# A K projection in two bank halves, and second scores and sums moved among the V quarters

## The chip, the cores and the metric

The kernel runs on one core of one Trainium2 chip. The metric is the device time of one execution in microseconds (us); before the change it was 892.15 us, the median of three runs (890.42 to 892.38).

## The reference, cut to what matters

The block has two parts. Part A is a segment-recurrent attention over 2048 tokens of width 512, with 32 heads of size 128. It walks through 64 segments of 32 tokens; each sees eight memory rows and its own tokens, and its first eight output rows are the memory of the next segment, so the segments must be done one after the other. Part B is a gated feed-forward block with a spatial mixing over all 2048 tokens. The attention loop is what matters here:

```
for s in range(n_seg):
    h = concat([mem, x[:, 32*s : 32*s+32]])      # 40 rows
    q, k, v = h @ Wq, h @ Wk, h @ Wv             # 32 heads of 128
    scores = where(mask, q @ k.T * scale, -1e9)
    p = softmax(scores)
    o = (p @ v) @ Wo
    mem = o[:, :8]
    outs.append(o[:, 8:])
```

## The kernel before

The kernel is a list of instructions for five engines, written out by hand in `fast_path`. A small emitter tracks which instruction reads and writes which token (a tile, or one of the eight PSUM banks) and places the semaphore waits; the order on each engine is the order of the calls. There is no scheduler: where a call stands in the step loop (line 869) is where its instructions stand in the queues of TensorE, ScalarE and VectorE.

The weights stay in SBUF. The projections of a step have only 32 rows, so each matmul uses a 128x32 column tile of the array, and four matmuls in four column tiles run side by side (the text calls them a quad). One projection of 16 heads is four quads of 512 columns, one for each 128 of the model width (`dc`). The step loop handles the heads in two halves, `b` 0 and 1:

- `QK(s, b, mi)` (L474) projects q (`mi` 0) or k (`mi` 1) of half `b` into bank 0, 1, 6 or 7 (`QKB`, L462). `QK_evac` (L485) copies the bank with ScalarE into `Tst` (L488), and VectorE transposes it in 32x32 blocks into `QT` (L494) or `KT` (L497).
- `S_half(s, b)` (L507) computes the scores into bank `b`: four mask matmuls (L511), which need no data of the step, then sixteen for the heads (L520) and four for the memory rows (L526).
- `sm_exp` (L532) is the exponential, `sm_sums` (L537) sums it with a matrix of ones (L541, L546), `sm_ln` (L553) and `sm_rcp` (L557) make the reciprocal on ScalarE, and `sm_norm` (L561, L566) multiplies it in on VectorE.
- `V_half(s, b, dcs)` (L569) projects v into bank 6 or 2; its four quads, one for each `dc`, are the V quarters, 0 to 3. `V_evac` (L579) copies the result, half 0 with VectorE (L584), half 1 with ScalarE (L582).
- `PV_half(s, b)` (L586) multiplies probabilities and values (L592, and L598 for the memory rows) into banks 0, 1, 6 and 7. Then follow `cT_evac` (L607), the output projection `Wo` (L619, matmuls L625), its copies `part_evac` (L636, ScalarE half L640), and `mem_out` (L644, matmuls L649), which brings the eight memory rows into the next step's `hT`.

Between the V quarters and PV stands a filler group of other work, where there is one (L942): in step 0 to 47 a group that prepares a later chunk, which is a V group of four quads (`vx_group`, L430) in steps 0 to 7, 14 and 15 and a Q or K group of sixteen 128x128 matmuls (L411) otherwise; in steps 49 to 62 a piece of part B's input projection (`z2_pre`, L725). Steps 48 and 63 have none.

The part of the step loop that the change touches reads before (arguments as in the code):

```
QK(s, 1, mi); QK_evac(s, 1, mi)      # mi = 0, then 1
S_half(s, 0); sm_exp(0)
V_half(s, 0); V_evac(0, "dve")       # four quarters
sm_sums(0); sm_ln(0)
S_half(s, 1); sm_exp(1); sm_rcp(0)
V_half(s, 1, (0, 1, 2))
sm_sums(1); sm_ln(1); sm_rcp(1)
V_half(s, 1, (3,)); V_evac(1, "act")
sm_norm(0); sm_norm(1)
```

Of the kernel before, what the change touches and what calls it, by code (L numbers as in the profile page):

```python
# [8 lines left out]
U32 = mybir.dt.uint32  # L9
# [160 lines left out]
def fast_path(nc, st, keep, A_x, A_mem0, A_Wq, A_Wk, A_Wv, A_Wo, A_seg_len, B_w_in, B_w_sp, B_b_sp, B_w_out, out):  # L170
# [9 lines left out]
    DC = D // 128  # L180
# [85 lines left out]
    def PB(b):  # L266
        return ("ps", b)
# [10 lines left out]
    def dve(fn, **k):  # L278
        return em.add("dve", fn, **k)
# [101 lines left out]
    def slot(s):  # L381
        return s % NSLOT
# [91 lines left out]
    def QK(s, b, mi, dcs=range(DC)):  # L474
# [3 lines left out]
        for dc in dcs:  # L478
            for c in range(4):
# [2 lines left out]
                                                           start=(dc == 0), stop=(dc == DC - 1), tile_position=(0, 32 * c)),  # L482
                   reads=[("hTx", (s // 4) % 3), ("hTm", s, dc // 2), ("W", mi, 2 * b), ("W", mi, 2 * b + 1)], writes=[PB(bank)])

    def QK_evac(s, b, mi):  # L485
        bank = QKB[(b, mi)]
        tb = mi
        act(lambda e: e.activation(out=Tst[:, tb, :].rearrange("p (hp i r) -> p hp i r", i=32, r=2),  # L488
                                   in_=ps[:, bank, :].rearrange("p (hp r i) -> p hp i r", r=2, i=32), func=ACT.Copy),
            reads=[PB(bank)], writes=[("T", tb)])  # L490
        src = Tst[:, tb, :].bitcast(U32)
        if mi == 0:
            dst = QT[:, b, :, :, :].rearrange("p hp q r -> p (hp q r)").bitcast(U32).rearrange("p (hp q) -> p hp q", hp=8)[:, :, 8:40]
            dve(lambda e: e.transpose(out=dst, in_=src), reads=[("T", tb)], writes=[("QT", b)])  # L494
        else:
            dst = KT[:, b, :, :, :].rearrange("p hp q r -> p (hp q r)").bitcast(U32)
            dve(lambda e: e.transpose(out=dst, in_=src), reads=[("T", tb)], writes=[("KT", b)])  # L497

    def qx_copy(s):
        j = s % CK  # L500
# [6 lines left out]
    def S_half(s, b):  # L507
        bank = SBK[b]
        for c in range(4):
            q = slice(32 * c, 32 * c + 32)  # L510
            pe(lambda e, q=q, c=c: e.matmul(ps[q, bank, 0:224], lhsT=ident[:, q], rhs=mask[:, :], start=True, stop=False,  # L511
                                            skip_group_check=True, tile_position=(0, 32 * c)),
               reads=["ident", "mask"], writes=[PB(bank)])
        j = s % CK
        buf = (s // CK) % 2
        rd = [("QT", b), ("KT", b), ("QTe", b)]
        for g in range(4):
            for c in range(4):
                hp, r = 2 * c + g // 2, g % 2
                pe(lambda e, hp=hp, r=r, c=c, g=g: e.matmul(  # L520
                    ps[32 * c:32 * c + 32, bank, g * 40:(g + 1) * 40], lhsT=KT[:, b, hp, :, r], rhs=QT[:, b, hp, :, r],
                    start=False, stop=(g == 3), skip_group_check=True, tile_position=(0, 32 * c)),
                    reads=rd, writes=[PB(bank)])
        for c in range(4):
            h0 = 16 * b + 4 * c
            pe(lambda e, c=c, h0=h0: e.matmul(  # L526
                ps[32 * c:32 * c + 32, bank, 160:224], lhsT=QTx[buf][:, 1, j, h0:h0 + 4, :].rearrange("p h k -> p (h k)"),
                rhs=QT[:, b, 2 * c:2 * c + 2, 0:16, :].rearrange("p hp q r -> p hp r q"),
                start=False, stop=True, skip_group_check=True, tile_position=(0, 32 * c)),
                reads=rd + [("QTx", buf, 1, i) for i in range(8)], writes=[PB(bank)])  # L530

    def sm_exp(b):  # L532
        bank = SBK[b]
        act(lambda e: e.activation(out=E_sb[:, b, :], in_=ps[:, bank, 0:224], func=ACT.Exp, scale=scale, bias=SHIFT),
            reads=[PB(bank)], writes=[("E", b), ("Ex", b)])
# [333 lines left out]
    for s in range(NSEG):  # L869
        j4 = s % 4  # L870
        rb = s // 4
        if j4 == 0 and rb > 0:
            load_h(rb - 1)
        if s == NSEG - 1:
            load_h(rb)
        if s % 2 == 1 and s // 2 < NWT:
            wT_piece(s // 2)
        if j4 == 0 and 2 <= rb + 2 < RB:
            load_x(rb + 2, 0)
        if s == 4:  # L880
            load_xe(3, 1)

        QK(s, 0, 0, (0, 1))
        if s > 0:
            mem_out(s - 1, 1)
        QK(s, 0, 1, (0, 1))
        QK(s, 0, 0, (2, 3))
        QK_evac(s, 0, 0)
        QK(s, 0, 1, (2, 3))
        QK_evac(s, 0, 1)  # L890
        for mi in range(2):
            QK(s, 1, mi)
            lastop["qk"[mi]] = em.by_eng["pe"][-1]
            QK_evac(s, 1, mi)
        if s == NSEG - 1:
            load_wT(0, [lastop["q"]])
        if s == 0:
            for n in range(2):
                start_v(n)
        S_half(s, 0)  # L900
        sm_exp(0)
        if s == 0:
            for n in range(2, 4):
                start_v(n)
        V_half(s, 0)
        V_evac(0, "dve")
        sm_sums(0)
        sm_ln(0)
        S_half(s, 1)
        lastop["s"] = em.by_eng["pe"][-1]  # L910
        sm_exp(1)
        sm_rcp(0)
        if s == 0:
            for n in range(4, 8):
                start_v(n)
        V_half(s, 1, (0, 1, 2))
        sm_sums(1)
        sm_ln(1)
        sm_rcp(1)
        V_half(s, 1, (3,))  # L920
        lastop["v"] = em.by_eng["pe"][-1]
        if s == NSEG - 1:
            sp(lambda e: e.dma_start(w_in1, winr[:, :, 0:FH]), writes=["w_in1"], after=[lastop["s"], lastop["x"]])
            sp(lambda e: e.dma_start(z2[:, 0:NP, :], z2p_d.rearrange("r p f -> p r f")),
               reads=[("z2p", r, hf) for r in range(NP) for hf in range(2)],
               writes=[("z2", r, hf) for r in range(NP) for hf in range(2)], after=[lastop["v"]])
            for r in range(8, RB - 2):
                xn2T_dma(r, [lastop["s"], lastop["x"]])
# [48 lines left out]
        if s == 8:  # L977
            ln_apply(1)
        if s == 12:
            xT(1, XB)  # L980
            late.append(lambda: xe_copy(3, XB))
        elif j4 == 0:
            late += gv.pour(1)
        if j4 == 1 and rb > 0:
            F_group(rb - 1, XB, True)
            F_add(rb - 1, XB)
        if j4 == 2 and 2 <= rb + 2 < RB:
            xT(0, XB)
            late.append(lambda: ring_copy(rb + 2, XB))
        for f in late:  # L990
            f()
        if s + 2 < NSEG:
            load_vx(s + 2)
        if j4 == 1 and rb >= 2:
            xn2_apply(rb - 2, rb % 2)
            xn2_store(rb - 2, rb % 2)
        if s == 3 * CK - 1:
            free0 = [lastop["s"], px]
            sp(lambda e: e.dma_start(w_in2, winr[:, :, FH:F]), writes=["w_in2"], after=free0)
        if 0 <= s - 3 * CK + 1 < 8:  # L1000
            xn2T_dma(s - 3 * CK + 1, free0)
        px = lastop.get("x")
# [956 lines left out]
```

## Time and profile before

| | |
|---|---|
| median of three runs | 892.15 us (890.42 to 892.38) |
| the profiled execution | 891.1 us |
| its span, first to last instruction | 889.4 us |
| mean granted TensorE clock | 0.994 |
| L481, the Q and K projections, busy | 240.5 us, 4096 matmuls |
| L575, the V projections, busy | 140.4 us, 2048 matmuls |
| L488, the Q and K evacuations on ScalarE, busy | 145.9 us, 256 instructions of 596 ns |
| L520, the scores, busy | 35.5 us, 2048 matmuls |
| L541 and L546, the sums, busy | 32.6 and 26.2 us |

The 64 steps take most of the span: the first scores of step 1 start at 63.68 us and those of step 63 at 708.31 us. Busy time on TensorE counts each matmul until its end, while the next one has long started. To see what one costs in a stream, take the distance between starts of successive rows in the timeline; a gap of a tenth of a microsecond does not show as idle time there.

### The profile page before, as it was taken

How to read it: one execution, taken by the hardware profiler on the slowest of the kernel's cores; microseconds unless marked ns; L12 is line 12 of the kernel's file. 1: busy time of each engine (PE TensorE's matmuls, PEld its weight loads, DVE VectorE, ACT ScalarE, POOL GpSimd, SP SyncE). 2: the span in 40 equal slices, each digit the busy share in tenths (PEclk: the TensorE clock that was granted, in tenths of full speed). 3: DMA queues.
4: the chain of work that ended last, by engine and by line, in shares of the span. 5: the costliest groups of instructions: out<-in, count | busy, mean ns of one | idle time of the engine just before them, and what ended most of it. 6: DMA issues, size and time to landing. Idle time of an engine off the chain costs nothing.

```text
span 889.4 us, 46102 instructions
## 1 busy us (share of the span) xinstructions
PE 862.0 (97%) x21213; PEld 487.0 (55%) x21213; DVE 487.4 (55%) x1127; ACT 455.5 (51%) x1145; POOL 110.7 (12%) x280
## 2 busy tenths in 40 slices
PE   6889999999999999999999999999999979999997
PEld 6645555555656555656665655555555534444443
DVE  3445556565656556565656565555555546464443
ACT  2346566666665666666665666565566655400000
POOL 1420111111111111010101111111101013100000
PEclk9999999999999999999999999999999999999999
DMA  9962222222320311211212122432221296032101
GB/s 326 376 180 52 63 57 60 43 60 63 60 58 25 83 45 37 60 54 43 60 42 57 49 61 79 73 73 67 65 61 56 76 273 227 1 100 76 62 13 38
DMA packets 106312, 74.55 MB, mean 84 GB/s; under 512 B 62360, under 2 KB 91616, under 8 KB 106112
## 3 DMA queue, kind: packets, MB, share of 16 engines
q1 hardware_dynamic: 105600, 71.27, 28.8%
q8 instruction: 168, 2.75, 1.3%
q14 instruction: 32, 0.26, 0.1%
q0 software_dynamic: 192, 0.20, 0.1%
q10 hardware_dynamic: 320, 0.07, 0.0%
HBM read 41.07 MB, written 20.22 MB: 69 GB/s over the span
## 4 chain that ended last, share of the span: by engine, by line
PE 93%; DVE 2%; DMA 2%; issue 1%; POOL 1%; ACT 0%; SPq 0%; DVEq 0%
PE f_ps L481 26%; PE f_ps L625 13%; PE f_ps L575 12%; PE f_ps L1064 11%; PE f_ps L411 7%; PE f_ps L676 4%; PE f_ps L592 3%; PE f_ps L430 3%; PE f_ps L1153 3%; PE f_ps L1057 2%; PE f_ps L725 2%; PE f_ps L520 2%; PE f_ps L541 1%; PE f_ps L511 1%; DMA f_arena<-in_B_w_in_dram 1%; PE f_ps L649 1%
## 5 line engine op out<-in xcount | busy, mean ns | idle before, releaser
L481 PE MATMUL f_ps<-f_arena,f_hT 128*32 128x512 bf16 x4096 | 240.5, 380 | 1.0 <-issue 0.4
L488 ACT ACTIVATE f_Tst<-f_ps 128x512 bf16<-128x512 f32 x256 | 145.9, 596 | 78.6 <-PE f_ps L481 78.3
L481 PEld LDWEIGHTS f_ps<-f_arena,f_hT 128*32 128x32 bf16 x4096 | 93.6, 96 | 104.6 <-ACT f_hT L654 33.3
L575 PE MATMUL f_ps<-f_arena,f_hT 128*32 128x512 bf16 x2048 | 140.4, 378 | 0.0
L625 PE MATMUL f_ps<-f_arena,f_cT 128*32 128x256 bf16 x4096 | 127.4, 272 | 0.8 <-ACT f_cT L611 0.8
L625 PEld LDWEIGHTS f_ps<-f_arena,f_cT 128*32 128x32 bf16 x4096 | 99.8, 96 | 24.1 <-ACT f_cT L611 22.1
L494 DVE STREAM_TRANSPOSE f_QT<-f_Tst 128x256 uint32<-128x256 uint32 x128 | 57.0, 445 | 92.4 <-ACT f_Tst L488 92.4
L1064 PE MATMUL f_ps<-f_arena 128*128 128x512 bf16 x448 | 100.1, 379 | 0.0
L613 DVE TENSOR_SCALAR f_cT<-f_ps 128x320 bf16<-128x320 f32 x128 | 56.9, 486 | 39.7 <-PE f_ps L598 39.7
L497 DVE STREAM_TRANSPOSE f_KT<-f_Tst 128x256 uint32<-128x256 uint32 x128 | 57.0, 445 | 29.1 <-ACT f_Tst L488 26.3
L1064 PEld LDWEIGHTS f_ps<-f_arena 128*128 128x128 bf16 x448 | 43.7, 98 | 52.6
L411 PE MATMUL f_ps<-f_hTe,f_arena 128*128 128x128 bf16 x1024 | 68.2, 225 | 4.2 <-DVE f_arena L422 3.2
L411 PEld LDWEIGHTS f_ps<-f_hTe,f_arena 128*128 128x128 bf16 x1024 | 60.6, 101 | 14.1 <-issue 9.2
L504 POOL COPY f_QT<-f_arena 128x256 bf16<-128x256 bf16 x64 | 30.8, 481 | 298.7 <-PE f_ps L526 298.6
L611 ACT ACTIVATE f_cT<-f_ps 128x320 bf16<-128x320 f32 x128 | 49.0, 435 | 36.8 <-PE f_ps L598 36.8
L561 DVE SCALAR_TENSOR_TENSOR f_E_sb<-f_R_sb,f_E_sb 128x160 bf16<-128x160 f32 x128 | 41.6, 325 | 46.3 <-ACT f_R_sb L557 46.3
L642 DVE CAST f_part<-f_ps 128x256 bf16<-128x256 f32 x64 | 27.2, 424 | 67.0 <-PE f_ps L625 67.0
L553 ACT ACTIVATE f_R_sb<-f_ps 128x160 f32<-128x160 f32 x128 | 38.8, 303 | 38.1 <-PE f_ps L546 38.1
L575 PEld LDWEIGHTS f_ps<-f_arena,f_hT 128*32 128x32 bf16 x2048 | 45.1, 95 | 21.1
L654 ACT ACTIVATE f_hT<-f_ps 128x16 bf16<-128x16 f32 x126 | 23.1, 183 | 55.4 <-PE f_ps L649 55.1
L633 POOL COPY f_cTx<-f_cT 128x256 bf16<-128x256 bf16 x64 | 25.6, 401 | 195.6 <-DVE f_cT L613 195.6
L1070 DVE TENSOR_TENSOR f_arena<-f_ps,f_arena 128x512 f32<-128x512 f32 x28 | 19.3, 689 | 55.8 <-PE f_ps L1064 55.8
(106 smaller groups left out, 1160.3 us busy)
## 6 DMA issues: line engine op xcount, KB each, us to landing
wT_d<-f_wst SPq DMA_DIRECT2D x32, 256.0 KB, 2.1
f_arena<-wT_d SPq DMA_DIRECT2D x32, 256.0 KB, 5.1
f_arena<-in_A_Wq_dram SPq DMA_DIRECT2D x4, 1024.0 KB, 8.5
f_arena<-in_A_Wk_dram SPq DMA_DIRECT2D x4, 1024.0 KB, 14.1
f_arena<-in_A_Wv_dram SPq DMA_DIRECT2D x4, 1024.0 KB, 14.5
f_arena<-in_A_Wo_dram SPq DMA_DIRECT2D x4, 1024.0 KB, 13.6
f_Vx<-vext_d SPq DMA_DIRECT2D x62, 64.0 KB, 2.8
vext_d<-f_Vs SPq DMA_DIRECT2D x24, 128.0 KB, 2.0
```

The lines of the kernel that those rows point to most:

```text
L411: pe(lambda e, h=h, dc=dc, hh=hh: e.matmul(ps[:, bank, hh * 128:(hh + 1) * 128], lhsT=ws[:, dc, h * DH:(h + 1) * DH], rhs=hTe[:, ck % 3, d ...
L481: pe(lambda e, dc=dc, c=c, rhs=rhs: e.matmul(ps[32 * c:32 * c + 32, bank, :], lhsT=hT[:, sl, dc, :], rhs=rhs, start=(dc == 0), stop=(dc == ...
L488: act(lambda e: e.activation(out=Tst[:, tb, :].rearrange("p (hp i r) -> p hp i r", i=32, r=2), in_=ps[:, bank, :].rearrange("p (hp r i) -> ...
L494: dve(lambda e: e.transpose(out=dst, in_=src), reads=[("T", tb)], writes=[("QT", b)])
L497: dve(lambda e: e.transpose(out=dst, in_=src), reads=[("T", tb)], writes=[("KT", b)])
L553: act(lambda e: e.activation(out=R_sb[:, b, :], in_=ps[:, bank, 224:384], func=ACT.Ln, scale=LNS), reads=[PB(bank)], writes=[("R", b)])
L561: dve(lambda e: e.scalar_tensor_tensor(out=E_sb[:, b, 0:160], in0=R_sb[:, b, :], scalar=RK, in1=E_sb[:, b, 0:160], op0=ALU.mult, op1=ALU.m ...
L575: pe(lambda e, dc=dc, c=c, c0=c0: e.matmul(ps[32 * c:32 * c + 32, bank, :], lhsT=hT[:, sl, dc, :], rhs=w_v[:, dc, c0:c0 + 512], start=(dc ...
L611: act(lambda e: e.activation(out=dst, in_=src, func=ACT.Copy, scale=UNSC), reads=[PB(PVB[c])], writes=[("cT", c)])
L613: dve(lambda e: e.tensor_scalar(out=dst, in0=src, scalar1=UNSC, scalar2=None, op0=ALU.mult), reads=[PB(PVB[c])], writes=[("cT", c)])
L625: pe(lambda e, h=h, g=g, i=i, b=b, c=c: e.matmul(ps[32 * g:32 * g + 32, bank, 0:d1 - d0], lhsT=cTh[:, i, 8:40], rhs=w_o[:, h, d0:d1], star ...
L1064: pe(lambda e: e.matmul(ps[:, bank, 0:TB], lhsT=z2[:, sc, fb * 128:(fb + 1) * 128], rhs=wTb[tb % 2][:, :, sc, :], start=(n == 0), stop=(n ...
```

## The change

The last projection of each step, K of half 1, is done in two pieces of eight heads. Each piece has four quads of 256 columns, a bank of its own (7 and 2), an evacuation of 256 columns and a transpose of 128 elements, each with its own token; the second scores read both tokens. The first V half is interrupted after three quarters: first sums, second scores, then quarter 3 and the first V evacuation. Of the second V half, two quarters stand in front of the second sums instead of three, and two behind.

```diff
+    KP = (7, 2)
+
+    def K_piece(s, p):
+        bank = KP[p]
+        sl = slot(s)
+        for dc in range(DC):
+            for c in range(4):
+                rhs = w_k[:, dc, :].rearrange("p (h c i) -> p c h i", c=4, i=32)[:, c, 16 + 8 * p:24 + 8 * p, :]
+                pe(lambda e, dc=dc, c=c, rhs=rhs: e.matmul(ps[32 * c:32 * c + 32, bank, 0:256], lhsT=hT[:, sl, dc, :], rhs=rhs,
+                                                           start=(dc == 0), stop=(dc == DC - 1), tile_position=(0, 32 * c)),
+                   reads=[("hTx", (s // 4) % 3), ("hTm", s, dc // 2), ("W", 1, 2 + p)], writes=[PB(bank)])
+        act(lambda e: e.activation(out=Tst[:, 1, 256 * p:256 * p + 256].rearrange("p (hp i r) -> p hp i r", i=32, r=2),
+                                   in_=ps[:, bank, 0:256].rearrange("p (hp r i) -> p hp i r", r=2, i=32), func=ACT.Copy),
+            reads=[PB(bank)], writes=[("T", 1, p)])
+        src = Tst[:, 1, 256 * p:256 * p + 256].bitcast(U32)
+        dst = KT[:, 1, 4 * p:4 * p + 4, :, :].rearrange("p hp q r -> p (hp q r)").bitcast(U32)
+        dve(lambda e: e.transpose(out=dst, in_=src), reads=[("T", 1, p)], writes=[("KT", 1, p)])
...
-        rd = [("QT", b), ("KT", b), ("QTe", b)]
+        rd = [("QT", b), ("QTe", b)] + ([("KT", 1, 0), ("KT", 1, 1)] if b else [("KT", 0)])
...
-        for mi in range(2):
-            QK(s, 1, mi)
-            lastop["qk"[mi]] = em.by_eng["pe"][-1]
-            QK_evac(s, 1, mi)
+        QK(s, 1, 0)
+        lastop["q"] = em.by_eng["pe"][-1]
+        QK_evac(s, 1, 0)
+        for p in range(2):
+            K_piece(s, p)
+        lastop["k"] = em.by_eng["pe"][-1]
...
-        V_half(s, 0)
-        V_evac(0, "dve")
+        V_half(s, 0, (0, 1, 2))
         sm_sums(0)
         sm_ln(0)
         S_half(s, 1)
         lastop["s"] = em.by_eng["pe"][-1]
         sm_exp(1)
+        V_half(s, 0, (3,))
+        V_evac(0, "dve")
         sm_rcp(0)
...
-        V_half(s, 1, (0, 1, 2))
+        V_half(s, 1, (0, 1))
         sm_sums(1)
         sm_ln(1)
         sm_rcp(1)
-        V_half(s, 1, (3,))
+        V_half(s, 1, (2, 3))
```

The rest of the diff splits the token of `Tst` in two halves, so that the other evacuations write, and their transposes read, both.

More of the change, by code (lines that the diff above doesn't have):

```diff
@@ L489, in QK_evac @@
                                    in_=ps[:, bank, :].rearrange("p (hp r i) -> p hp i r", r=2, i=32), func=ACT.Copy),
-            reads=[PB(bank)], writes=[("T", tb)])
+            reads=[PB(bank)], writes=[("T", tb, 0), ("T", tb, 1)])
         src = Tst[:, tb, :].bitcast(U32)
@@ L493, in QK_evac @@
             dst = QT[:, b, :, :, :].rearrange("p hp q r -> p (hp q r)").bitcast(U32).rearrange("p (hp q) -> p hp q", hp=8)[:, :, 8:40]
-            dve(lambda e: e.transpose(out=dst, in_=src), reads=[("T", tb)], writes=[("QT", b)])
+            dve(lambda e: e.transpose(out=dst, in_=src), reads=[("T", tb, 0), ("T", tb, 1)], writes=[("QT", b)])
         else:
             dst = KT[:, b, :, :, :].rearrange("p hp q r -> p (hp q r)").bitcast(U32)
-            dve(lambda e: e.transpose(out=dst, in_=src), reads=[("T", tb)], writes=[("KT", b)])
+            dve(lambda e: e.transpose(out=dst, in_=src), reads=[("T", tb, 0), ("T", tb, 1)], writes=[("KT", b)])
     def qx_copy(s):
```

## The prediction

> **What bounds the kernel now.** The page comes first: how full TensorE is, and who owns the chain that ends last.
>
> ```profile
> span 889.4 us, 46102 instructions
> PE 862.0 (97%) x21213; PEld 487.0 (55%) x21213; DVE 487.4 (55%) x1127; ACT 455.5 (51%) x1145; POOL 110.7 (12%) x280
> PE 93%; DVE 2%; DMA 2%; issue 1%; POOL 1%; ACT 0%; SPq 0%; DVEq 0%
> ```
>
> TensorE owns the end. Its 97% says little about small waits, since a matmul is drawn until its modelled end while the next already runs. So I read the starts in TensorE's timeline. Step 35 is typical of the 64. Four matmuls in four column tiles start together; I call them a quad.
>
> ```profile
> 414.85 3.22 PE L481 MATMUL f_ps<-f_arena,f_hT 128*32 128x512 bf16 x56
> 417.89 0.27 PE L511 MATMUL f_ps<-f_mask,f_ident 128*32 128x224 bf16 x4
> ...
> 418.09 0.20 PE L526 MATMUL f_ps<-f_QT,f_arena 128*32 128x64 bf16 x4
> 418.12 1.04 PE L575 MATMUL f_ps<-f_arena,f_hT 128*32 128x512 bf16 x16
> 419.02 0.25 PE L541 MATMUL f_ps<-f_E_sb,f_ones 128*32 128x160 bf16 x4
> ...
> 419.12 0.27 PE L511 MATMUL f_ps<-f_mask,f_ident 128*32 128x224 bf16 x4
> 419.25 0.28 PE L520 MATMUL f_ps<-f_QT,f_KT 128*32 128x40 bf16 x16
> 419.36 0.20 PE L526 MATMUL f_ps<-f_QT,f_arena 128*32 128x64 bf16 x4
> 419.39 0.82 PE L575 MATMUL f_ps<-f_arena,f_hT 128*32 128x512 bf16 x12
> 420.05 0.25 PE L541 MATMUL f_ps<-f_E_sb,f_ones 128*32 128x160 bf16 x4
> ...
> 420.15 0.39 PE L575 MATMUL f_ps<-f_arena,f_hT 128*32 128x512 bf16 x4
> 420.48 0.51 PE L411 MATMUL f_ps<-f_hTe,f_arena 128*128 128x128 bf16 x6
> ```
>
> The 14 quads from 414.85 to 417.89 take 0.217 us each. The V quads take 0.216. So there are three small waits in this stretch. The first four V quads last 0.90 instead of 0.864: sums 0 waits 0.03 for its exponential. The second scores last 0.27 (419.12 to 419.39), the first 0.23 (417.89 to 418.12): 0.04 for the second K transpose. The second sums wait under 0.01 (0.66 against 0.65). ScalarE and VectorE confirm the first two.
>
> ```profile
> 417.25 0.60 ACT L488 ACTIVATE f_Tst<-f_ps 128x512 bf16<-128x512 f32 x1 [0.21 <-PE f_ps L481]
> 418.12 0.60 ACT L488 ACTIVATE f_Tst<-f_ps 128x512 bf16<-128x512 f32 x1 [0.27 <-PE f_ps L481]
> 418.61 0.35 ACT L534 ACTIVATE f_E_sb<-f_ps 128x224 bf16<-128x224 f32 x1
> ```
> ```profile
> 417.88 0.45 DVE L494 STREAM_TRANSPOSE f_QT<-f_Tst 128x256 uint32<-128x256 uint32 x1 [0.36 <-ACT f_Tst L488]
> 418.75 0.45 DVE L497 STREAM_TRANSPOSE f_KT<-f_Tst 128x256 uint32<-128x256 uint32 x1 [0.42 <-ACT f_Tst L488]
> 419.21 0.69 DVE L584 CAST f_V_sb<-f_ps 128x512 bf16<-128x512 f32 x1
> ```
>
> The exponential ends at 418.96, and sums 0 starts at 419.02. The K transpose ends at 419.20, and the second scores' L520 starts at 419.25. The exponential starts with no idle time before it: it queued behind the K evacuation, though its scores could have reached it at about 418.35 (L526's 418.09 + 0.20, and 0.06 to reach ScalarE; from the last K matmul's end, 414.85 + 3.22 = 418.07, to its evacuation it is 0.05).
>
> A larger wait stands behind it, in steps whose filler group before PV is short. There PV's second half starts late.
>
> ```profile
> 577.52 0.27 PE L592 MATMUL f_ps<-f_E_sb,f_V_sb 32*128 32x40 bf16 x16
> 577.65 0.21 PE L598 MATMUL f_ps<-f_E_sb,f_Vx 32*128 32x64 bf16 x4
> 577.87 0.28 PE L592 MATMUL f_ps<-f_E_sb,f_V_sb 32*128 32x40 bf16 x16
> ```
> ```profile
> 576.90 0.34 ACT L557 ACTIVATE f_R_sb<-f_R_sb 128x160 f32<-128x160 f32 x1
> 577.14 0.58 ACT L582 ACTIVATE f_V_sb<-f_ps 128x512 bf16<-128x512 f32 x1
> ```
> ```profile
> 67.26 0.21 PE L598 MATMUL f_ps<-f_E_sb,f_Vx 32*128 32x64 bf16 x4
> 67.48 0.28 PE L592 MATMUL f_ps<-f_E_sb,f_V_sb 32*128 32x40 bf16 x16
> ...
> 555.91 0.21 PE L598 MATMUL f_ps<-f_E_sb,f_Vx 32*128 32x64 bf16 x4
> 556.68 0.28 PE L592 MATMUL f_ps<-f_E_sb,f_V_sb 32*128 32x40 bf16 x16 [0.56 <-DVE f_E_sb L566]
> ```
> ```profile
> 400.87 0.21 PE L598 MATMUL f_ps<-f_E_sb,f_Vx 32*128 32x64 bf16 x4
> 401.00 0.28 PE L592 MATMUL f_ps<-f_E_sb,f_V_sb 32*128 32x40 bf16 x16
> ```
> ```profile
> PEld f_ps L592 <- issue: 9.6, 25, 0.4
> ```
>
> Undisturbed, the halves lie 0.13 apart (400.87 to 401.00); here it is 0.22 (577.65 to 577.87, and 67.26 to 67.48), a wait of 0.09. The second V evacuation ends at 577.72; 0.05 of signalling and a weight load of about 0.1 later the matmuls start. The list of waits calls this "issue", 25 times. That fits the program: 14 steps with a z2 group, 9 of the first 16 with a V group (step 0 left aside), and 2 with nothing (48 and 63), where the gap is 0.77, so 0.64 too much.
>
> **The change part by part.**
>
> *The K projection in two pieces*: 4 quads of 512 columns become 8 of 256, with 16 more matmuls and 16 more weight loads per step. The output projection runs the same shape with the same 128x32 weights:
>
> ```profile
> 401.89 1.70 PE L625 MATMUL f_ps<-f_arena,f_cT 128*32 128x256 bf16 x56
> 403.43 0.21 PE L649 MATMUL f_ps<-f_G_sb,f_part 128*32 128x8 bf16 x8
> ```
>
> 14 quads in 1.54 is 0.110 each. Before: 4 x 0.217 = 0.87; after: 8 x 0.110 = 0.88, +0.01 per step. K starts at 414.85 + 10 x 0.217 = 417.02, so the pieces finish issuing at 417.46 and 417.90.
>
> *The evacuations.* One of 512 becomes two of 256, on ScalarE ahead of the first exponential.
>
> ```profile
> L640 ACT ACTIVATE f_part<-f_ps 128x256 bf16<-128x256 f32 x64 | 24.5, 383 | 46.0 <-PE f_ps L625 46.0
> ```
>
> A 256-wide one lasts 0.38. Followed at once by another instruction, a 512-wide one occupies the engine for 0.49 of its 0.60 (418.12 to 418.61), an overlap of 0.10. I take 0.28 for 256; without overlap it is 0.38. ScalarE is free of the Q evacuation at 417.25 + 0.49 = 417.74. Piece 0 is there before that (last quad 417.35 + 0.01; a 256-wide matmul lasts 1.70 - 13 x 0.110 = 0.27; then 0.06: 417.69), so it goes 417.74 to 418.12. Piece 1 is there at 417.79 + 0.01 + 0.27 + 0.06 = 418.13 and goes to 418.51; the engine is free at 418.41. The scores reach it at 418.36. So the first exponential starts at 418.41, not 418.61, and ends at 418.76.
>
> *V quarter 3 moved behind the second scores.* Sums 0 now has three V quads ahead of it: 418.13 + 0.65 = 418.78, while the exponential is through at 418.76 + 0.05 or 0.06 = 418.82. The wait is 0.04, about 0.01 more than now. The cover shrank by 0.22 and the exponential came 0.20 earlier: the edit is hidden by its own other half, and if the exponential does not come earlier, it costs nearly all of the 0.22.
>
> *The second scores' wait.* Neither engine shows a 128-element transpose. The nearest rows put it between a 64-element VectorE operation and the 256-element transpose itself (0.45):
>
> ```profile
> 420.25 0.33 DVE L561 SCALAR_TENSOR_TENSOR f_E_sb<-f_R_sb,f_E_sb 128x160 bf16<-128x160 f32 x1 [0.35 <-ACT f_R_sb L557]
> 420.49 0.22 DVE L566 SCALAR_TENSOR_TENSOR f_E_sb<-f_R_sb,f_E_sb 128x64 bf16<-128x64 f32 x1
> ```
>
> 96 elements cost 0.11 there, so halving 256 saves about 0.14: I take 0.31. The last piece's transpose then runs from 418.54 to 418.85, and L520 of the second scores could start at 418.90. Its turn comes at 418.82 + 0.11 + 0.10 = 419.03. The wait of 0.04 goes, with 0.13 to spare.
>
> *Sums 1 between two V quarters.* Ahead of it, three quads still follow the second scores (V quarter 3 of half 0, two of half 1), the same cover of 0.65 for the same second exponential: no change in that wait. Sums 1 comes 0.01 + 0.23 + 0.65 + 0.04 + 0.11 + 0.23 + 0.65 = 1.92 after the step's first L511 would have started, against 420.05 - 417.89 = 2.16: 0.24 earlier. Behind it stand Ln, reciprocal and second V evacuation on ScalarE and the normalisation on VectorE, all of which PV's second half needs. ScalarE was held by this row, not by the last V quad: V evacuation 577.14 follows the reciprocal 576.90 by 0.24, with no idle time. So the evacuation ends near 577.48, and PV's second half can start at 577.63, before its turn at about 577.76. The 0.09 goes in 23 steps, and the two bare steps gain 0.24 each. The first V evacuation on VectorE starts 0.39 later (its last quad moved from 418.77 to 419.16), ends at 420.29 instead of 419.90, and pushes nothing but the first normalisation, by a few hundredths (420.25): no cost, as the filler keeps PV off until 421.
>
> *Banks and queues.* Piece 1 uses bank 2, which the second V half needs from about 419.37; the piece is evacuated by 418.51. No DMA is issued within the moved lines except in the last step (the w_in1 load waits for the second scores, which come 0.2 earlier). The order on ScalarE, VectorE, GpSimd and SyncE keeps its sequence.
>
> *Sum.* Per step -0.04 + 0.01 + 0.01 = -0.02, over 63 steps -1.3; 23 x -0.09 = -2.1; 2 x -0.24 = -0.5; together -3.9 us. The profiled execution took 891.1 us (span 889.4 and 1.7 around it), 1.05 under the median of 892.15. Taken off that median: 888.2 us.
>
> **The rivals.**
>
> *A. ScalarE comes too late (slower).* Two evacuations without overlap: piece 0 until 418.12, piece 1 from 418.13 to 418.51, and only then the exponential, 0.10 later than forecast. Each step then waits that much more at sums 0: 63 x 0.10 = 6.3, net +2.4, 894.5. The sum turns at an exponential that starts at 418.47 (0.06 x 63 = 3.9) and is slower by over 0.2% from 418.50. For it: no row has two 256-wide evacuations of this interleaved output back to back. Against: L488's own overlap of 0.10. [...]
>
> *B. The halved transpose costs as much as the whole.* With 0.36 from one to the next and 0.45 for the last (417.88 + 2 x 0.36 + 0.45 = 419.05), L520 starts at 419.11 instead of 419.03. 63 x 0.08 = 5.0, net +1.1: 893.3, within 0.2%.
>
> *C. PV's wait stays*, because something else ends it than the evacuation: only 1.3 + 0.5 remain, 890.4, just within 0.2%. For it: the profile names "issue". Against: the 0.15 from the evacuation's end is what signalling and a weight load take.
>
> *D. The first exponential starts with its scores (418.36)*: sums 0 wait nothing, another 0.05 x 63 = 3.2: 885.0. It would need evacuations shorter than I took.
>
> *E. The added weight loads are not hidden.*
>
> ```profile
> 419.01 0.10 PEld L541 LDWEIGHTS f_ps<-f_E_sb,f_ones 128*32 128x32 bf16 x4 [0.35 <-ACT f_E_sb L534]
> ```
>
> Four loads side by side take 0.10; four more such groups per step are 0.40, 64 x 0.40 = 26 us, net +22: 914. The 0.110 quads of L625 already contain theirs and speak against it. [...]
>
> **How the numbers follow.** Forecast 0.55, A 0.15, B 0.08, C 0.09, D 0.11, E 0.02. About 0.2% (1.8 us) is what a measurement of this kernel can tell from no change. Faster: forecast and D, 0.66. Same: B and C, 0.17. Slower: A and E, 0.17. The range runs from D (885.0) to B (893.4) and leaves out A and E.
>
> **What would show it.** Right: in an ordinary step the exponential (L552 in the changed kernel) starts about 0.51 after the first scores' L529, and the second scores take 0.23; the PV halves lie 0.13 apart in the z2 steps; steps 1 to 63 are shorter by some 0.02, the z2 steps by 0.11. Wrong: V's first three quads last over 0.75 until sums 0 (A), the second scores over 0.27 (B), the gap in the z2 steps stays at 0.22 (C), the two K pieces take over 0.95 together (E).

## The result, and the profile after

The changed kernel takes 895.05 us (median of 18 runs, 891.07 to 897.64) against 892.14 us of the kernel before (18 runs, 889.84 to 894.68): ratio 1.0028 with a 95% interval of 1.0016 to 1.0040. Its median is 2.9 us higher, where 888.2 was forecast and 893.4 was the end of the range. The profiled execution took 894.11 us with a span of 892.4, at the same granted clock as before (0.994).

The page of the changed kernel, by the span, the engines, the instruction queue and the owners of the chain:

```profile
span 892.4 us, 48270 instructions
...
PE 862.1 (97%) x22230; PEld 512.7 (57%) x22237; DVE 485.8 (54%) x1191; ACT 458.1 (51%) x1209; POOL 110.3 (12%) x280
...
q8 instruction: 176, 2.88, 1.4%
...
PE 94%; DMA 2%; issue 1%; DVE 1%; ACT 1%; POOL 0%; DVEq 0%; SPq 0%
```

TensorE's busy time is the same to 0.1 us and it still owns the chain; it just takes 3 us longer. The line to notice is the third, which I had not quoted before the change. There it reads:

```profile
q8 instruction: 168, 2.75, 1.3%
```

Next, where the time went. The first scores' mask matmuls mark each step in TensorE's timeline. Here are those of step 1 and of step 63 after, and then before.

```profile
63.72 0.27 PE L529 MATMUL f_ps<-f_mask,f_ident 128*32 128x224 bf16 x4
...
711.11 0.27 PE L529 MATMUL f_ps<-f_mask,f_ident 128*32 128x224 bf16 x4
```
```profile
63.68 0.27 PE L511 MATMUL f_ps<-f_mask,f_ident 128*32 128x224 bf16 x4
...
708.31 0.27 PE L511 MATMUL f_ps<-f_mask,f_ident 128*32 128x224 bf16 x4
```

Steps 1 to 62 take 647.39 instead of 644.63: the 2.8 us are there, and the rest of the span differs by 0.2. But a typical step is *shorter*, as forecast. Here are TensorE, ScalarE and VectorE of the changed kernel in step 33, an ordinary one (a Q or K group as its filler; a V-filler step has a V group there, a z2 step a piece of part B's input projection).

```profile
401.67 0.27 PE L529 MATMUL f_ps<-f_mask,f_ident 128*32 128x224 bf16 x4
401.90 0.82 PE L593 MATMUL f_ps<-f_arena,f_hT 128*32 128x512 bf16 x12
402.58 0.25 PE L559 MATMUL f_ps<-f_E_sb,f_ones 128*32 128x160 bf16 x4
402.69 0.27 PE L529 MATMUL f_ps<-f_mask,f_ident 128*32 128x224 bf16 x4
...
402.92 0.82 PE L593 MATMUL f_ps<-f_arena,f_hT 128*32 128x512 bf16 x12
403.59 0.25 PE L559 MATMUL f_ps<-f_E_sb,f_ones 128*32 128x160 bf16 x4
403.69 0.61 PE L593 MATMUL f_ps<-f_arena,f_hT 128*32 128x512 bf16 x8
404.23 1.07 PE L411 MATMUL f_ps<-f_hTe,f_arena 128*128 128x128 bf16 x16
```
```profile
401.52 0.76 ACT L496 ACTIVATE f_Tst<-f_ps 128x256 bf16<-128x256 f32 x2
402.18 0.35 ACT L552 ACTIVATE f_E_sb<-f_ps 128x224 bf16<-128x224 f32 x1
```
```profile
401.90 0.38 ACT L496 ACTIVATE f_Tst<-f_ps 128x256 bf16<-128x256 f32 x1
```
```profile
402.02 0.60 DVE L501 STREAM_TRANSPOSE f_KT<-f_Tst 128x128 uint32<-128x128 uint32 x2
```

The row of 401.90 is the second of the two evacuations by itself: it starts 0.38 after the first and 0.28 before the exponential. The exponential starts 0.51 after the first scores (401.67 to 402.18), three V quads then last 0.68 (401.90 to 402.58), and the second scores take 0.23 (402.69 to 402.92). In a z2 step the PV halves lie 0.13 apart instead of 0.22:

```profile
622.94 0.21 PE L616 MATMUL f_ps<-f_E_sb,f_Vx 32*128 32x64 bf16 x4
623.07 0.28 PE L610 MATMUL f_ps<-f_E_sb,f_V_sb 32*128 32x40 bf16 x16
```

So the longer time must lie in some steps only. I took as the undisturbed length of a kind of step the lower quartile of its steps, and call what the steps last beyond it "stops" (step 48, which has no filler, is in none of the three kinds):

| | ordinary step | V-filler step | z2 step | steps 1 to 62 | stops in them |
|---|---|---|---|---|---|
| before | 10.366 | 10.323 | 10.279 | 644.63 | 3.4 |
| after | 10.349 | 10.167 | 10.167 | 647.39 | 10.1 |

Undisturbed, the steps are 3.9 us shorter (2.8 - 6.7). The stops add 6.7. Each such figure is of one profiled execution: a second one of the changed kernel, below, has 5.8 us of stops instead of 10.1, so a difference of a few us between the stops of two kernels says little by itself. A stop looks like this in TensorE's timeline of the changed kernel:

```profile
415.83 0.24 PE L610 MATMUL f_ps<-f_E_sb,f_V_sb 32*128 32x40 bf16 x10
416.51 0.22 PE L610 MATMUL f_ps<-f_E_sb,f_V_sb 32*128 32x40 bf16 x6 [0.44 <-issue]
```

It cuts one operation of 16 equal matmuls after the tenth: the eleventh reads the same tiles as the tenth (f_E_sb, f_V_sb) and, by the program's tokens, needs nothing that the tenth did not have. Others cut other lines, mostly in mid-operation:

```profile
106.34 0.20 PE L544 MATMUL f_ps<-f_QT,f_arena 128*32 128x64 bf16 x1 [0.42 <-issue]
...
122.53 0.24 PE L376 MATMUL f_ps<-f_ident,f_xn 128*32 128x128 bf16 x4 [0.50 <-issue]
...
131.74 0.39 PE L430 MATMUL f_ps<-f_arena,f_hTe 128*32 128x512 bf16 x1 [0.52 <-issue]
...
282.17 0.39 PE L679 MATMUL f_ps<-f_part,f_F_sb 128*32 128x512 bf16 x2 [0.80 <-issue]
...
335.56 0.34 PE L376 MATMUL f_ps<-f_ident,f_xn 128*32 128x128 bf16 x10 [0.93 <-issue]
```

The kernel before has them too, but fewer:

```profile
164.26 0.29 PE L376 MATMUL f_ps<-f_ident,f_xn 128*32 128x128 bf16 x6 [0.60 <-issue]
```

What they share is seen by counting. Here TensorE's busy time in stretches of the changed kernel, each from one stop to another; the number behind x counts matmuls.

```profile
core 0: us, PE busy (x), PEclk, DMA share, GB/s
106.30:122.50 16.20, 15.69 (x509) 1.00 0.20 49
122.50:131.71 9.21, 8.51 (x255) 1.00 0.29 69
...
207.70:212.55 4.85, 4.39 (x128) 1.00 0.42 71
...
269.26:282.14 12.88, 12.08 (x383) 1.00 0.09 29
```

509, 255, 128 and 383 are 4, 2, 1 and 3 times 127.5. In steps 1 to 62 I found 20 stops inside an operation, and all 19 stretches between them are a multiple of 127.5 matmuls to within two. The page counts 22230 matmuls and 22237 weight loads, one for each, so 127.5 matmuls are 255 instructions. The change adds 64 x 16 matmuls and as many weight loads, 2048 instructions, and the instruction queue q8 has 176 - 168 = 8 packets more: 256 for each. It moved 2.88 MB in 176 packets, 16.4 KB each. I take 256 instructions for one packet, an estimate from these counts; why a stretch counts 255, one fewer, no view shows.

The two also keep step with each other. Between the first stop shown and the one at 582.35, the last of the 20, TensorE and q8 show:

```profile
106.34:582.35 476.01, 470.86 (x14907) 1.00 0.23 55
```
```profile
q8 instruction: 117, 1.92, 1.7%
```

14907 / 117 is 127.4 matmuls for one packet. From each of the 20 stops to the next, exactly as many packets start as there are pieces: 18 have started by the stop at 106.34, 94 by that at 416.51 (9683 matmuls later, 76 x 127.4), 135 by that at 582.35.

This gave a theory, **refill**: each packet of q8 (16.4 KB) brings TensorE a piece of 256 instructions, and TensorE stops at a border when the next piece is not there. The counts suggest it; no view names what a stopped TensorE waits for, the profile says "issue". In the same time, more instructions make more borders and shorter pieces: 647.4 us hold 19313 matmuls before and 20212 after, so a piece lasts 4.27 us on average before (647.4 / 19313 x 127.5) and 4.08 after. The **rival**: the stops have nothing to do with the instructions' number; the loss comes from the new order among the V quarters, or from chance of where the transfers of part B fall.

Part B has a large transfer that matters here. In every second step SyncE issues a transposing DMA of a piece of `w_sp` (`wT_piece`, L762 after) and stores the result. Here the DMA view of the changed kernel around the stop at 416.51, in three stretches: 412.0 to 412.9, 412.9 to 413.9 and 413.9 to 414.3.

```profile
q1 hardware_dynamic: 307, 0.10, 41.9%
...
f_wst<-in_B_w_sp_dram SPq DMA_TRANSPOSE x1, 5.1
```
```profile
q1 hardware_dynamic: 777, 0.20, 111.8%
```
```profile
q1 hardware_dynamic: 66, 0.01, 14.8%
q8 instruction: 1, 0.02, 14.2%
```

In the second stretch the transpose's small packets (777 of some 260 bytes) fill the 16 engines, their times adding up to 111.8% of what the engines have, and q8's packet starts behind nearly all of them, at 414.05. The stop ends 2.5 later. For 17 of the 20 stops the distance from the last instruction packet's start is 2.2 to 3.0 us, for the other three, all under 0.3 long, 3.1 to 3.6. The median is 2.6, and the next packet starts 1.04 us after a stop at the earliest, 1.2 in the median. By my estimate a piece needs about 3.8 us (1.2 + 2.6, from these 20 stops), against the 4.08 that it lasts on average in the changed kernel and the 4.27 before.

### The profile page after: what moved, and what is told of

It is laid out like the page before. It is cut to its first block, busy times and chain, and to the rows that moved or that the text cites. A ratio compares the mean times of both kernels' runs of the same rounds, so it can differ in the third digit from the quotient of the medians.

```text
span 892.4 us, 48270 instructions
## 1 busy us (share of the span) xinstructions
PE 862.1 (97%) x22230; PEld 512.7 (57%) x22237; DVE 485.8 (54%) x1191; ACT 458.1 (51%) x1209; POOL 110.3 (12%) x280
## 3 DMA queue, kind: packets, MB, share of 16 engines
q1 hardware_dynamic: 105600, 71.27, 28.6%
q8 instruction: 176, 2.88, 1.4%
## 4 chain that ended last, share of the span: by engine, by line
PE 94%; DMA 2%; issue 1%; DVE 1%; ACT 1%; POOL 0%; DVEq 0%; SPq 0%
PE f_ps L481 19%; PE f_ps L643 13%; PE f_ps L593 12%; PE f_ps L1085 11%; PE f_ps L411 7%; PE f_ps L493 6%; PE f_ps L694 4%; PE f_ps L430 3%; PE f_ps L610 3%; PE f_ps L743 3%; PE f_ps L1078 3%; PE f_ps L1174 2%; PE f_ps L559 2%; PE f_ps L538 1%; PE f_ps L529 1%; DMA f_arena<-xn_d 1%
## 5 line engine op out<-in xcount | busy, mean ns | idle before, releaser
L481 PE MATMUL f_ps<-f_arena,f_hT 128*32 128x512 bf16 x3072 | 185.5, 380 | 0.6
L593 PE MATMUL f_ps<-f_arena,f_hT 128*32 128x512 bf16 x2048 | 142.1, 378 | 0.1
L506 ACT ACTIVATE f_Tst<-f_ps 128x512 bf16<-128x512 f32 x192 | 107.8, 596 | 61.4 <-PE f_ps L481 61.4
L481 PEld LDWEIGHTS f_ps<-f_arena,f_hT 128*32 128x32 bf16 x3072 | 66.8, 95 | 75.7 <-ACT f_hT L672 32.6
L602 DVE CAST f_V_sb<-f_ps 128x512 bf16<-128x512 f32 x64 | 44.3, 692 | 48.7 <-PE f_ps L593 48.7
L493 PE MATMUL f_ps<-f_arena,f_hT 128*32 128x256 bf16 x2048 | 67.6, 273 | 0.0
L493 PEld LDWEIGHTS f_ps<-f_arena,f_hT 128*32 128x32 bf16 x2048 | 55.5, 97 | 14.2
```

The source lines that it names most:

```text
L481: pe(lambda e, dc=dc, c=c, rhs=rhs: e.matmul(ps[32 * c:32 * c + 32, bank, :], lhsT=hT[:, sl, dc, :], rhs=rhs, start=(dc == 0), stop=(dc == ...
L493: pe(lambda e, dc=dc, c=c, rhs=rhs: e.matmul(ps[32 * c:32 * c + 32, bank, 0:256], lhsT=hT[:, sl, dc, :], rhs=rhs, start=(dc == 0), stop=(d ...
L593: pe(lambda e, dc=dc, c=c, c0=c0: e.matmul(ps[32 * c:32 * c + 32, bank, :], lhsT=hT[:, sl, dc, :], rhs=w_v[:, dc, c0:c0 + 512], start=(dc ...
L602: dve(lambda e: e.tensor_copy(out=V_sb[:, b, :], in_=ps[:, bank, :]), reads=[PB(bank)], writes=[("V", b)])
```

## The experiments

The kernels under one of the three headings below ran on the same chip, beside the kernel before. Gains and losses in us are worked out from the ratios.

### Parts of the change alone, and the instruction number alone

**The K pieces without the new V order.** From the changed kernel:

```
-        V_half(s, 0, (0, 1, 2))
+        V_half(s, 0)
+        V_evac(0, "dve")
...
-        V_half(s, 0, (3,))
-        V_evac(0, "dve")
...
-        V_half(s, 1, (0, 1))
+        V_half(s, 1, (0, 1, 2))
...
-        V_half(s, 1, (2, 3))
+        V_half(s, 1, (3,))
```

> K of half 1 in two pieces, the V order as before. Undisturbed steps get shorter by about 0.07 us (no wait at sums 0, none at the second scores, 0.01 for the pieces), the PV gap in the z2 steps stays at 0.22: -4.4 us in all. Theory refill (TensorE stops where a 16 KB piece of 256 of its own instructions ends and the next has not landed; 32 more instructions a step let each piece last shorter; worth about +6.8 us in the changed kernel): about +2.4, 894.5. Rival (the moved V quarters or sums cost the time): 887.7.

Measured: 889.11 us, ratio 0.9991 (0.9979 to 1.0003), between the two expectations. TensorE's timeline of this kernel:

```profile
407.32 1.03 PE L593 MATMUL f_ps<-f_arena,f_hT 128*32 128x512 bf16 x16
408.18 0.24 PE L559 MATMUL f_ps<-f_E_sb,f_ones 128*32 128x160 bf16 x4
...
408.28 0.27 PE L529 MATMUL f_ps<-f_mask,f_ident 128*32 128x224 bf16 x4
...
408.51 0.81 PE L593 MATMUL f_ps<-f_arena,f_hT 128*32 128x512 bf16 x12
```

Four V quads take 0.86 and the second scores 0.23: with the old order the earlier exponential takes both small waits away. The ordinary step lasts 10.308, shorter than in the changed kernel (10.349): there the new V order gave back most of it, since sums 0 lost a quad of cover. By its undisturbed steps this kernel would gain 4 us or so (38 ordinary steps x 0.058, 9 V-filler steps x 0.096, 14 z2 steps x 0.056, step 48 another 0.2 to 0.5); it gained 0.8. That added stops take the other 3 us is worked out by subtraction; its profile has 5.0 us of stops, 1.6 more than that of before, which is half of it.

**The new V order without the K pieces.** In the kernel before:

```
-        V_half(s, 0)
-        V_evac(0, "dve")
+        V_half(s, 0, (0, 1, 2))
         sm_sums(0)
...
+        V_half(s, 0, (3,))
+        V_evac(0, "dve")
...
-        V_half(s, 1, (0, 1, 2))
+        V_half(s, 1, (0, 1))
...
-        V_half(s, 1, (3,))
+        V_half(s, 1, (2, 3))
```

> The V order of the change, K in one piece as before: TensorE has exactly as many instructions as before. The first exponential still starts behind the 512-wide evacuation, so sums 0 wait about 0.2 us a step: +12.6, and the PV waits go: -2.6; about +10, 902. Theory refill: stops at piece borders stay near the 4 us of before. Rival (the order brings the stops): another +7, 909.

Measured: 902.72 us, ratio 1.0141 (1.0123 to 1.0159): 12.5 us more, nearer the 10 of refill than the 17 of the rival. TensorE and ScalarE of this kernel show why: the exponential comes late, and three V quads are not enough cover (0.90 from the first to sums 0, against 0.65 for three quads).

```profile
412.97 0.82 PE L575 MATMUL f_ps<-f_arena,f_hT 128*32 128x512 bf16 x12
413.87 0.25 PE L541 MATMUL f_ps<-f_E_sb,f_ones 128*32 128x160 bf16 x4
```
```profile
413.46 0.35 ACT L534 ACTIVATE f_E_sb<-f_ps 128x224 bf16<-128x224 f32 x1
```

The ordinary step grows by 0.21 to 10.579; the prediction had priced exactly this, "nearly all of the 0.22", for an exponential that does not come earlier. The stops are 2.8 us, no more than before, with 168 instruction packets as before. So the new order alone, without added instructions, costs waits but adds no stops. That is no clean proof against the rival, since in steps that are 0.21 longer each piece has more time too.

**As many instructions, no other change.** In the kernel before, Q of half 1 is computed in matmuls of 256 columns, into the same bank, with the same evacuation:

```
-            for c in range(4):
-                rhs = ws[:, dc, :]...[:, c, 16 * b:16 * b + 16, :]
-                pe(lambda e, ...: e.matmul(ps[32 * c:32 * c + 32, bank, :], lhsT=hT[:, sl, dc, :], rhs=rhs, ...
+            for hf in range(2 if b == 1 and mi == 0 else 1):
+                for c in range(4):
+                    n = 16 // (2 if b == 1 and mi == 0 else 1)
+                    rhs = ws[:, dc, :]...[:, c, 16 * b + n * hf:16 * b + n * hf + n, :]
+                    pe(lambda e, ...: e.matmul(ps[32 * c:32 * c + 32, bank, 32 * n * hf:32 * n * hf + 32 * n], lhsT=hT[:, sl, dc, :], rhs=rhs, ...
```

> The kernel before, only the Q projection of half 1 issued as 256-column matmuls into the same bank: 16 more matmuls and 16 more weight loads a step, no other instruction, no other order, no other wait. Theory refill: +0.6 for the narrower quads and about +6.8 of stops at piece borders, 899.5. Rival (pieces, banks, evacuations or the order cost it): +0.6, 892.7.

Measured: 891.99 us, ratio 1.0020 (1.0007 to 1.0032). An ordinary step, 10.375, is 0.01 longer, which the 256-wide shape costs by itself, at most 0.6 us over the kernel. The other 1.2 of the 1.8 us would be stops (4.5 us in its profile, 1.1 more than before). The loss is nearer to the rival's 0.6 than to the 7.4 that I expected of refill, though clear of no change. Instructions alone, at this number, do not make 6.7 us.

**The whole change, in steps 48 to 63 only** (from the changed kernel):

```
+        new = s >= 3 * CK
+        if new:
+            for p in range(2):
+                K_piece(s, p)
+        else:
+            QK(s, 1, 1)
+            QK_evac(s, 1, 1)
...
-        V_half(s, 0, (0, 1, 2))
+        V_half(s, 0, (0, 1, 2) if new else range(DC))
```

and likewise for the other V quarters.

> The whole change, but only in steps 48 to 63; steps 0 to 47 as before. In steps 49 to 62 the z2 filler has 4 matmuls where the Q or K filler has 16, so even with the pieces TensorE has only 8 instructions more than an ordinary step of before. Theory refill: the steady gain of 0.11 us in 14 steps and about 0.4 in the bare ones stays, stops change little: about -2, 890.2. Rival (each changed step costs 0.1 on the mean): -2.0 + 16 x 0.11 = -0.3, 891.9.

Measured: 887.99 us, ratio 0.9976 (0.9966 to 0.9986): faster than before by 2.1 us, and two instruction packets more (170, for 512 instructions). The z2 steps have the changed kernel's length (10.173) and the earlier steps the old one, with 2.4 us of stops. The gain per step that I forecast is real where the added stops are few.

### With and without the transposes

The changed kernel was run again beside these, without any edit.

> The changed kernel once more, beside the experiments on one chip, since the kernel before took 892.1 us in the first comparison and 890.0 us in the second. If the chips differ only by a constant: +2.9 over before. If the delay of the instruction pieces differs by chip, the loss is smaller here, nearer to the +2.7 of stops that the pieces alone showed: about -1 against before.

Measured: 890.84 us, ratio 1.0009 (0.9993 to 1.0025): the loss is smaller in this comparison, 0.8 us, which the interval doesn't tell from none, with 5.8 us of stops. That is the yardstick for the next two. In both, part B's weights are not transposed: the loads take `w_sp` as it is, so the spatial mixing works with other numbers and the steps have no transposing DMA and no store of its result.

```
-        if s % 2 == 1 and s // 2 < NWT:
-            wT_piece(s // 2)
...
-            sp(lambda e, t=t: e.dma_start(wTb[tb % 2][:, t, :, :], wT_d[8 * tb + t]), ...
+            sp(lambda e, t=t: e.dma_start(wTb[tb % 2][:, t, :, :], B_w_sp[(8 * tb + t) * 64:(8 * tb + t + 1) * 64, :].rearrange(
+                "a (b rb c) -> (a b) rb c", b=2, c=64)), ...
```

The changed kernel so:

> The changed kernel without the 32 transposing DMAs of the spatial weight and their stores (the loads of the transposed weight read the untransposed one, so the spatial mixing uses another matrix). They are the largest bursts on the DMA engines during the steps. Theory refill, with pieces late because they queue behind bursts: most of the stops go, and the steps keep their steady 10.35 and 10.17 us; steps 1 to 62 take about 641 us instead of 647. Rival (the stops are not a matter of DMA): steps 1 to 62 stay at 647.

The kernel before so:

> The kernel before with the same left out. Theory refill: its about 3.4 us over the undisturbed steps shrink to 1 or less, steps 1 to 62 take about 641.5 to 642 us; set against this one, the changed kernel without the transposes is then faster by its steady 3.5. Rival: the changed one stays slower by 2.9.

Measured: 885.51 us for the changed kernel (ratio to the kernel before as it stands 0.9953, 0.9936 to 0.9969), 888.18 for the kernel before (0.9983, 0.9963 to 1.0003). Without the transposes the change makes the kernel 2.7 us *faster*, toward the 3.9 of the forecast (every run of it is below the median of the other); with them, on the same chip, 0.8 slower. By the ratios, leaving them out saves the changed kernel 5.0 us and the kernel before 1.5. Steps 1 to 62 of the changed kernel take 640.75, as refill expected (641); those of the kernel before take 643.87, where it expected at most 642. The stops in the steps fall from 5.8 to 3.4 in the changed kernel and are 1.6 in the kernel before, where 1 or less was expected. The changed kernel's instruction queue is the same with and without (176 packets). So this traffic costs the changed kernel some 3.5 us more than the kernel before (from four ratios, each known to 1.5 us or so), as much as the loss and more; it is not the only source of stops, since 3.4 us of them remain.

**K pieces in all steps, the new V order from step 48 on** (where PV waits):

```
+        new = s >= 3 * CK
...
-        V_half(s, 0, (0, 1, 2))
+        V_half(s, 0, (0, 1, 2) if new else range(DC))
```

> K in two pieces in all steps, the moved V quarters only from step 48. Sum of the earlier runs: pieces alone -0.9, the change from step 48 on -2.0, of which the pieces' own gain in those steps (16 x 0.056 = 0.9) counts twice: about -2. If the stops that the pieces add hit the ordinary steps as on average (+0.04 a step against -0.058): -2.7.

Measured: 887.66 us, ratio 0.9983 (0.9968 to 0.9999). Its undisturbed steps are the best of all (10.306 ordinary, 10.167 z2), but its profile has 3.9 us of stops where the late version has 2.4, and its gain of 1.5 us is not told from the 2.1 there. On the same chip it beats the changed kernel by 2.3 us. So with the pieces in place, the new V order in steps 0 to 47 costs these 2.3: about 1.5 by the undisturbed steps beside it (an ordinary one 10.356 in the changed kernel's second profile against 10.306 here, a V-filler one 10.18 against 10.22).

### More instructions, and shorter bursts

**Both Q projections in 256 columns**, 64 instructions per step more than before: the diff of the one-half version with `if mi == 0` in place of `if b == 1 and mi == 0`.

> The kernel before with both Q projections issued as 256-column matmuls into their banks: 32 more matmuls and 32 more weight loads a step, twice what one Q projection added. Theory refill: 1.2 for the narrower quads and more than twice the 1.4 of stops, since the pieces of 256 instructions last 0.35 us less: +4 to +6 against before. Rival (instructions do not matter): +1.2.

Measured: 907.07 us, ratio 1.0181 (1.0163 to 1.0199), 16.1 us more: the rival's 1.2 is out, and refill's 4 to 6 is missed by far too. The page of this kernel has 16 packets more than before for its 64 x 64 = 4096 additional instructions, again 256 for each:

```profile
span 901.4 us, 50191 instructions
...
q8 instruction: 184, 3.01, 1.4%
```

An ordinary step is only 0.03 longer (10.392), but the stops are 11.7 us in the profiled execution, and 32 of them cut an operation, against 8 in the kernel before and 20 in the changed one (stops of 0.06 us or more at a border). The borders are the same:

```profile
192.40:200.44 8.04, 7.93 (x256) 1.00 0.14 47
200.44:212.14 11.70, 11.30 (x383) 1.00 0.11 29
...
390.24:398.24 8.00, 7.98 (x255) 1.00 0.21 61
```

By count a piece lasts 3.93 us here (20980 matmuls in the 647.4 us). Against the kernel before, whose pieces last 4.27, the version with half of these instructions lost 1.8 us, this one 16.1 (by the ratio): twice the instructions, nine times the loss.

**The transposes in halves**, one in every step instead of one whole in every second, in the changed kernel, the late version and the kernel before:

```
-    def wT_piece(i):
-        sp(lambda e: e.dma_start_transpose(out=wst[:, :, :], in_=B_w_sp[i * 64:(i + 1) * 64, :]), writes=["wst"])
...
+    def wT_half(i, k):
+        h = RB // 2
+        sp(lambda e: e.dma_start_transpose(out=wst[:, h * k:h * k + h, :], in_=B_w_sp[i * 64:(i + 1) * 64, 64 * RB * k:64 * RB * (k + 1)]),
+           writes=[("wst", k)])
...
-        if s % 2 == 1 and s // 2 < NWT:
-            wT_piece(s // 2)
+        wT_half(s // 2, s % 2)
```

> The changed kernel with the spatial weight transposed in halves: a 64x1024 transpose and its store in every step instead of a 64x2048 one in every second. The same bytes in bursts half as long. Theory refill with queueing behind bursts: a packet of instructions is held up half as long, stops shrink, -1 to -2.5 against the changed kernel, that is about -0.5 against before. Rival: no change, +0.8.

> The change from step 48 on, and the transposes in halves. Theory refill: -2.0 from the first and up to -1 from the second, -2.5 to -3 against before. Rival: -2.

> The kernel before with the transposes in halves, to tell what the halves do without the change. Theory refill: its stops (about 3.4 us over the undisturbed steps, of which 1.3 went with the transposes taken out) shrink by some 0.5 to 1: about -0.7. Rival: 0.

Measured: 892.24 us (ratio 1.0002, 0.9987 to 1.0017), 892.68 (1.0018, 1.0004 to 1.0032) and 892.93 (1.0020, 1.0008 to 1.0032). The second and the third miss both expectations. The first lies between its two, and its interval holds both (-0.5 and +0.8), so it decides nothing. I thought that bursts half as long would be over before they delay a piece. With halves the late version and the kernel before are slower than the kernel before as it stands, and the changed kernel is left 0.2 over it, with 9.6 us of stops in its profile. The page of the kernel before with halves shows one difference, more packets for the same bytes (the second line is that of the changed kernel, whose transposes are whole, as before):

```profile
q1 hardware_dynamic: 111232, 71.28, 28.4%
```
```profile
q1 hardware_dynamic: 105600, 71.27, 28.6%
```

They took 28.4% of the engines' time against 28.6%, so the packets' number is not shown to be the cause. Twice as many bursts may also meet twice as many pieces; that was not measured by itself.

## Why the prediction was wrong

**What bounds the kernel** was right: TensorE owns the end, and the waits that I found were there. The gap of 0.22 in front of PV's second half was read rightly: it went to 0.13. The list of 25 "issue" waits beside it was misread. They are idle time of the weight loads in front of PV's *first* half (0.37 at 577.52 below, where the second half's loads at 577.84 have none), they include step 0 and a stop at 463.5 and leave out the two bare steps, and after the change the same idle time is still there (0.37 at 622.81, with L584 named instead); the match with 14 + 9 + 2 was chance. Other "issue" waits stood in the trace of before, as the one at 164.26 in the middle of an operation, and I gave them no cause and no price.

```profile
577.52 0.17 PEld L592 LDWEIGHTS f_ps<-f_E_sb,f_V_sb 32*128 32x128 bf16 x16 [0.37 <-issue]
...
577.84 0.15 PEld L592 LDWEIGHTS f_ps<-f_E_sb,f_V_sb 32*128 32x128 bf16 x9
```

**The evacuations and the exponential**: right. Forecast 0.51 after the first scores, measured 0.51; the two evacuations lie 0.38 apart and the exponential 0.28 behind the second, as chosen. Rival A fell.

**Sums 0**: forecast a wait of 0.04, measured 0.68 against 0.65, 0.03.

**The second scores' wait**: right, 0.27 to 0.23. Both halved transposes take 0.60 together, so one costs about 0.30 (forecast 0.31). Rival B fell. 

**PV's wait**: right, 0.22 to 0.13; V-filler and z2 steps are shorter by 0.16 and 0.11, forecast 0.11. Rival C fell. Rival D too, since sums 0 still waits.

**The sum of these**: for steps 1 to 62 the forecast is 62 x 0.02 + 23 x 0.09 + 0.24 = 3.55 us, and their undisturbed lengths fell by 3.9. Every term that I named was right to half a us.

**The failed step** is the first, "*the K projection in two pieces* ... with 16 more matmuls and 16 more weight loads per step", costed at "+0.01 per step". That is the time of the array, and of the array it is true: the two pieces take 0.87 (400.80 to 401.67 in step 33), the time of four quads of 512 columns (4 x 0.217), and rival E, which priced the loads at 0.40 per step on the array, fell. What the step left out is the instructions' own traffic: 32 more per step came with 8 packets more on q8, 176 against 168. The sum had no term for that, and no rival stood for it; in the profiled execution it was 6.7 us of added stops over 62 steps, against a gain of 3.9. How much of these the added instructions cause by themselves, and how much their meeting the transposes and the new order, the runs don't divide. Two things in the profile of before could have led to it: q8's 168 packets, one for every 253 matmuls and weight loads (2 x 21213 / 168), and a stop inside an operation (0.60 at 164.26).

What is shown, then: the stops inside operations lie multiples of 127.5 matmuls apart (all 19 stretches), with one instruction packet to each 127.5; the packets' number follows the number of added instructions, one for every 256 (168 packets, 170 for 512 more, 176 for 2048, 184 for 4096); the new order without the instructions adds no stops, in steps that it makes longer; more instructions without the new order lose time, +1.8 us for 32 a step and +16.1 for 64; and without part B's transposes the same change gains 2.7 us. The rival, order alone, falls as the whole cause: alone it loses through waits that the changed kernel does not have, and more instructions lose time without it. It has a part in the loss, though: with the pieces in place it costs 2.3 us in steps 0 to 47. Chance falls with the counts.

What stays open: whether and why the changed kernel stops for longer than the others with as many instructions (5.8 and 10.1 us in its two profiles, against 5.0 and 3.9 with the old V order in all steps or up to step 47, and 4.5 with Q in 256 columns). Where dense stretches fall against the borders is an argument, not a measurement. The loss was +2.5 us (by the ratio) in the first comparison and +0.8 in the second; the intervals overlap, so whether the two differ is open. What delays a piece where no other transfer runs, as ahead of 282.17, was not found. A version with this order and fewer TensorE instructions was not tried.

Of the versions that compute the same, the change in steps 48 to 63 alone has the lowest ratio, 0.9976, 2.1 us faster than before (the one with pieces in all steps, 0.9983, is not told from it), where the changed kernel was slower by 0.8 and 2.5.

## What to carry to other kernels

Where TensorE has no slack, as here at 97% busy, price an edit twice: in the array's time (with Q in 256 columns +0.01 us for an undisturbed step) and in the number of instructions (32 more per step cost +1.8 us, 64 more +16.1). In this kernel a stretch divided by its number of instructions in units of 256, the count of these runs, gave 4.27 us for a piece before and 4.08 after, close to the estimated 3.8 that one needs. If operations are already cut in the middle with "issue" as the reason (8 times in the kernel before), do not take the splitting of a matmul in two for free because its load is hidden; here it was not free. And apply a change of order only in the steps whose wait it removes: in steps 48 to 63 alone this change had the ratio 0.9976, in all steps 1.0028 and 1.0009.

## What the runs showed of the hardware that I had not expected

- q8 moved 2.88 MB in 176 packets of 16.4 KB, and had one packet more for every 256 TensorE instructions added (8 for 2048, 16 for 4096, 2 for 512). All 19 stretches between the 20 stops inside operations of the changed kernel are multiples of 127.5 matmuls, to within two; the stops in the steps lasted 0.1 to 1.1 us. In these 20 a stop ends 2.6 us in the median after the start of the last instruction packet, and the next packet starts 1.2 us in the median after the stop.
- With pieces of 4.27, 4.08 and 3.93 us on average the profiled stops were 3.4, 3.9 to 10.1, and 11.7 us. The busy share of TensorE, 97% before and after the change, did not show the difference.
- The kernel before took longer with its transposes in halves, 111232 packets instead of 105600 for 71.3 MB: ratio 1.0020 (1.0008 to 1.0032).
- In step 33 of the changed kernel a 256-wide evacuation of an interleaved output lasts 0.38, and the exponential behind it starts after 0.28 (401.90 to 402.18); its last scores end at 402.07. The two evacuations themselves lie 0.38 apart: the last matmul ahead of the second starts at 401.57 and lasts 0.27.
